# A grouped-query attention kernel: 480 rows of the output projection's weights loaded early through five transfer engines, the rest behind the last V block

## Chip, cores and metric

One core of a Trainium2 chip. The metric is device time of one execution in microseconds (us). The four runs of the kernel before agree within 0.2% (190.00 to 190.34 us).

## The reference, cut

```python
B, Sq, D = 8, 4, 512;  Hq, Hkv, Sk, Dh = 32, 8, 2048, 128      # all bf16
q = (x @ wq)                          # x: 32 tokens x 512, wq: 512 x 4096
scores = q . k_cache * Dh ** -0.5     # four query heads share one K/V head
o = softmax(scores) . v_cache         # k_cache, v_cache: 32 MiB each
return o.reshape(B, Sq, Hq * Dh) @ wo # wo: 4096 x 512, 4 MiB
```

## The kernel before: what the change and the argument touch

K and V come in 32 blocks of 1 MiB each, through one queue, into 7 and 6 buffers. Units are pairs of K/V heads: `p` is the head pair (four of them, `G2 = 4`), `b` the batch. The four quarters of `wo` belong to the four head pairs. `wo_sb` takes the buffer of `wq_sb`, so it can be loaded only after the queries are made. The trace shows sixteen completion increments for every load of 128 partitions; I read them as one for each of the core's sixteen transfer engines.

```python
def load_wo(p, r0, n):                 # r0..r0+n of 8 rows per partition
    rows = wo[p * HP * 128 : (p + 1) * HP * 128, :].rearrange("(q r) j -> q r j", r=WR)
    nc.sync.dma_start(wo_sb[:, p, r0 : r0 + n, :], rows[:, r0 : r0 + n, :])

load_k(0); <wq>; <x>
for u in range(NU + KA):               # the order of the loads
    if 0 < u < NU:                       loads.append(("k", u))
    if u >= KA - 1 and u - KA + 1 < NU:  loads.append(("v", u - KA + 1))
    if u in (NU, NU + 1):                # first quarter and half of the second
        loads.append(("wo", (u - NU, 0, WR if u == NU else 4)))
# ... [cut] identities, transposes of x and K, queries, scores, values ...
for step in range(-L - 1, NH):         # NH = 64 half blocks
    # ... [cut]
    if step == NH - 1 - 2 * VB:          # behind the last V block
        load_wo(1, 4, 4)
        load_wo(2, 0, WR)
        load_wo(3, 0, 4); load_wo(3, 4, 2); load_wo(3, 6, 2)
    if step == NH - 5:   project(0, 0, WR)
    elif step == NH - 3: project(1, 0, 4)
to_tokens(3);  project(1, 4, 4);  to_wo_rows(3)
project(2, 0, WR);  project(3, 0, 4);  project(3, 4, 2);  project(3, 6, 2)
# ... [cut] two copies (VectorE, ScalarE) and two stores
```

`project(p, r0, n)` is one matmul for each row of a partition and each half of the 512 output columns: `project(2, 0, WR)` is 16 matmuls.

The softmax here doesn't subtract the row's maximum and nothing guards it: scores larger than these inputs give would overflow.

## Time and profile before

| | before |
|---|---|
| time, median of 4 runs | 190.18 us (190.00 to 190.34) |
| span of the profiled run | 188.3 us |
| 1 MiB load of the third wo quarter lands | 181.68 us |
| last load of wo lands | 184.16 us |
| after that 1 MiB landing | 32 matmuls 3.67 us, a copy 0.36 us, the store |
| bytes read from memory | 72 MiB |

The prediction below shows the lines of the page. Two things are needed to read them. The span is shorter than the time of a run (187.7 against 189.51 us in the changed kernel's profiled run), because it counts from the first to the last instruction of the profile. And a load of 128 partitions has landed with the last of its sixteen completion increments (for the third wo quarter at 181.68 us, and its matmuls start at 181.72); the differences between the increments show how far the engines are apart. Where I print such differences, they come from these completion records, in an ordinary block.

### The profile page before, as it was taken

How to read it: one execution, taken by the hardware profiler on the slowest of the kernel's cores; microseconds unless marked ns; L12 is line 12 of the kernel's file. 1: busy time of each engine (PE TensorE's matmuls, PEld its weight loads, DVE VectorE, ACT ScalarE, POOL GpSimd, SP SyncE). 2: the span in 40 equal slices, each digit the busy share in tenths (PEclk: the TensorE clock that was granted, in tenths of full speed). 3: DMA queues.
4: the chain of work that ended last, by engine and by line, in shares of the span. 5: the costliest groups of instructions: out<-in, count | busy, mean ns of one | idle time of the engine just before them, and what ended most of it. 6: DMA issues, size and time to landing. Idle time of an engine off the chain costs nothing.

```text
span 188.3 us, 6428 instructions
## 1 busy us (share of the span) xinstructions
PE 154.9 (82%) x2861; PEld 141.9 (75%) x2892; DVE 113.3 (60%) x220; ACT 86.3 (46%) x170; POOL 1.1 (1%) x8
## 2 busy tenths in 40 slices
PE   0706597799999999998888889998885999998783
PEld 0605497699999898898888878887774988987572
DVE  6801544577777677767666668676664477673420
ACT  2011546665655666446554544454553464461000
POOL 2000000000000000000000000000000000000000
PEclk9985869999999999999999999999999699999999
DMA  6999999999999999999999999999999999999950
GB/s 251 425 438 393 418 430 426 423 428 425 419 425 421 426 421 423 430 419 423 431 421 421 430 423 421 425 426 425 423 421 428 425 426 423 426 424 416 422 207 10
DMA packets 10539, 75.97 MB, mean 403 GB/s; under 512 B 1200, under 2 KB 1296, under 8 KB 1936
## 3 DMA queue, kind: packets, MB, share of 16 engines
q1 hardware_dynamic: 10464, 75.55, 95.6%
q8 instruction: 22, 0.36, 0.7%
q14 instruction: 5, 0.04, 0.1%
q10 hardware_dynamic: 48, 0.02, 0.0%
HBM read 75.53 MB, written 0.03 MB: 401 GB/s over the span
## 4 chain that ended last, share of the span: by engine, by line
DMA 81%; PE 12%; ACT 3%; DVE 2%; issue 1%; SPq 1%; DVEq 0%
DMA k_sb<-in_k_cache_dram 64%; DMA wo_sb<-in_wo_dram 9%; DMA x_sb<-in_x_dram 7%; PE kp L161 3%; PE s_ps L222 3%; PE psq L185 2%; PE out_ps L314 2%; DVE kt L168 1%; ACT kt L166 1%; PE o_ps L246 1%; DVE q_bd L209 1%; ACT q_bd L209 1%; ACT probs L232 1%; PE l_ps L260 0%; PE pse L200 0%
## 5 line engine op out<-in xcount | busy, mean ns | idle before, releaser
L161 PE MATMUL kp<-ident,k_sb 128*128 128x128 f32 x512 | 83.1, 290 | 13.4 <-DMA k_sb<-in_k_cache_dram 13.4
L168 DVE COPY kt<-kp 128x1024 bf16<-128x1024 bf16 x96 | 65.3, 682 | 25.6 <-PE kp L161 24.9
L232 ACT ACTIVATE probs<-s_ps 64x256 bf16<-64x256 f32 x128 | 48.4, 378 | 66.3 <-PE s_ps L222 65.5
L161 PEld LDWEIGHTS kp<-ident,k_sb 128*128 128x128 f32 x512 | 56.7, 146 | 14.4 <-issue 14.1
L222 PE MATMUL s_ps<-q_bd,kt 128*128 128x64 bf16 x1024 | 43.3, 195 | 3.1 <-ACT kt L166 1.9
L222 PEld LDWEIGHTS <-kt 128*128 128x128 bf16 x1024 | 40.7, 100 | 4.9 <-ACT kt L166 2.2
L246 PEld LDWEIGHTS <-v_sb 128*128 128x128 bf16 x1024 | 34.4, 96 | 9.6 <-DMA v_sb<-in_v_cache_dram 2.4
L268 DVE TENSOR_REDUCE l_sb<-l_ps 128x32 f32<-128x512 f32 x32 | 22.1, 692 | 24.0 <-PE l_ps L260 21.7
L246 PE MATMUL o_ps<-probs,v_sb 128*128 128x32 bf16 x1024 | 35.1, 177 | 1.2 <-DMA v_sb<-in_v_cache_dram 1.1
L166 ACT COPY kt<-kp 128x1024 bf16<-128x1024 bf16 x32 | 32.4, 1012 | 8.1 <-PE kp L161 7.3
L260 PE MATMUL l_ps<-probs,ones 128*128 128x512 bf16 x33 | 12.4, 380 | 1.5
L272 DVE RECIPROCAL r_sb<-l_sb 128x32 f32<-128x32 f32 x32 | 11.3, 353 | 1.1
L314 PE MATMUL out_ps<-wo_sb,oP 128*32 128x256 bf16 x64 | 7.6, 272 | 0.8 <-DMA wo_sb<-in_wo_dram 0.8
L314 PEld LDWEIGHTS <-oP 128*32 128x32 bf16 x64 | 6.1, 96 | 1.5 <-issue 0.6
L367 ACT CAST out_sb<-out_ps 32x256 bf16<-32x256 f32 x1 | 0.4, 362 | 14.5 <-PE out_ps L314 14.5
L277 DVE TENSOR_TENSOR oT_all<-o_ps,r_sb 128x32 bf16<-128x32 f32 x32 | 5.8, 182 | 1.7 <-PE o_ps L246 1.5
L260 PEld LDWEIGHTS <-ones 128*128 128x128 bf16 x64 | 6.0, 98 | 0.8 <-issue 0.4
L176 PE MATMUL xtp<-ident,x_sb 32*128 32x32 bf16 x4 | 0.5, 191 | 6.6 <-DMA x_sb<-in_x_dram 6.4
L176 PEld LDWEIGHTS <-x_sb 32*128 32x128 bf16 x4 | 0.3, 114 | 7.1 <-DMA x_sb<-in_x_dram 6.8
L192 ACT ACTIVATE qT_all<-psq 128x256 bf16<-128x256 f32 x4 | 1.5, 386 | 8.7 <-PE psq L185 8.7
L209 DVE CAST q_bd<-pse 64x512 bf16<-64x512 f32 x4 | 2.6, 683 | 4.2 <-PE pse L200 4.2
L179 DVE COPY xT_sb<-xtp 128x32 bf16<-128x32 bf16 x4 | 0.5, 170 | 7.0 <-PE xtp L176 7.0
(23 smaller groups left out, 33.3 us busy)
## 6 DMA issues: line engine op xcount, KB each, us to landing
k_sb<-in_k_cache_dram SPq DMA_DIRECT2D x32, 1024.0 KB, 19.6
v_sb<-in_v_cache_dram SPq DMA_DIRECT2D x32, 1024.0 KB, 19.6
wq_sb<-in_wq_dram SPq DMA_DIRECT2D x1, 4096.0 KB, 14.2
wo_sb<-in_wo_dram SPq DMA_DIRECT2D x2, 1024.0 KB, 18.5
wo_sb<-in_wo_dram SPq DMA_DIRECT2D x3, 512.0 KB, 17.2
wo_sb<-in_wo_dram SPq DMA_DIRECT2D x2, 256.0 KB, 13.2
x_sb<-in_x_dram SPq DMA_DIRECT2D x1, 32.0 KB, 14.0
out_dram<-out_sb SPq DMA_DIRECT2D x1, 16.0 KB, 1.4
```

Of the source, the lines that this page charges most:

```text
L161: nc.tensor.transpose(kp[:, j, :], k4[:, w : w + 128], ident4[:, :])
L166: nc.scalar.copy(out=kt2, in_=kp2)
L168: nc.vector.tensor_copy(out=kt2, in_=kp2)
L209: (nc.scalar.copy if g else nc.vector.tensor_copy)(out=q_bd[rows, p, :, :, g, :], in_=pse[rows, :, :, :])
L222: nc.tensor.matmul(s_ps[:, 2 * j : 2 * j + 2, :], lhsT=k_t[:, j % (HC // 4), :, e], rhs=q_bd[:, p, e, b, :, :], start=(e == 0), stop=(e == 1),
L232: nc.scalar.activation(out=pr[rows, hf * HC : (hf + 1) * HC, cols], in_=s_ps[rows, :, cols], func=EXP)
L246: nc.tensor.matmul(o_ps[u][:, :], lhsT=vs[u][:, cc, :], rhs=pr[:, cc, :], start=(cc == 0), stop=(cc == C - 1),)
L260: nc.tensor.matmul(l_ps[:, :, :], lhsT=ones[:, :], rhs=pr[:, c : c + LC, :], start=(c == 0), stop=(c + LC == C),)
L268: nc.vector.tensor_reduce(out=l_sb[:, :], in_=l_ps[:, :, :].rearrange("d c q -> d q c"), axis=AX, op=ADD)
L272: nc.vector.reciprocal(r_sb[:, :], l_sb[:, :])
L277: nc.vector.tensor_tensor(out=oT_all[:, p * HP : (p + 1) * HP, b, :], in0=o_ps[u][:, :].rearrange("d (h s) -> d h s", h=HP), in1=r_sbs[u][ ...
L314: nc.tensor.matmul(out_ps[half][:, :], lhsT=oP[p][:, r, :], rhs=wo_sb[:, p, r, half * DH : (half + 1) * DH], start=(p == 0 and r == 0), st ...
```

## The change

The intent: the sixteen transfer engines drift apart during the run (increments 0.64 us apart at the third K block, 4.94 at the last load of wo), one more of them falling back by some 1.5 us at each of the first eight 16 KiB instruction fetches, and the end of the kernel waits for the slowest. So the first quarter of `wo` is used as ballast. Of its 1024 rows, 480 are loaded by eight small loads between the first K blocks, each of only 5 partitions and meant for only five engines; the rest goes behind the last V block. The early rows are projected in the middle of the kernel.

```diff
+    NE, WE, WM = 40, 12, 4                     # 40 partitions x 12 rows, 128 x 4, 32 x 1
+    wo_e = const.tile([64, WE, D], BF16, name="wo_e")
+    def load_wo_e(i):                          # five partitions, 12 KiB in each
+        hi, m = divmod(i, 4)
+        rows = wo[: NE * WE, :].rearrange("(q r) j -> q r j", r=WE)
+        a, b = hi * 32 + m, hi * NE // 2 + m
+        nc.sync.dma_start(wo_e[a : a + 17 : 4, :, :], rows[b : b + 17 : 4, :, :])
 ...
     for u in range(NU + KA):
+        if 1 <= u <= 8:
+            loads.append(("e", u - 1))
 ...
-        if u in (NU, NU + 1):
-            loads.append(("wo", (u - NU, 0, WR if u == NU else 4)))
 ...
+    nc.gpsimd.memset(wo_e[:, :, :], 0.0)       # ahead of the identities
     load_ready(0, 0)
 ...
         if step == NH - 1 - 2 * VB:
-            load_wo(1, 4, 4)
+            nc.sync.dma_start(wo_n[:, :], wo[HP * 128 - 32 : HP * 128, :])
+            load_wo_m()
+            load_wo(1, 0, WR)
             load_wo(2, 0, WR)
 ...
-        if step == NH - 5:
-            project(0, 0, WR)
-        elif step == NH - 3:
-            project(1, 0, 4)
+        if 28 <= step < 36:
+            e, r = divmod(step - 28, 4)
+            project_early(1 - e, r * 3, 3)
+        if step == 31:
+            nc.vector.tensor_copy(out=early[:, :], in_=out_e[:, 1, :])
     to_tokens(3)
-    project(1, 4, 4)
+    project(0, 0, WM + 1)
     to_wo_rows(3)
+    project(1, 0, WR)
     project(2, 0, WR)
 ...
-    nc.scalar.copy(out=out_sb[1][:, :], in_=out_ps[1][:, :])
+    nc.vector.tensor_tensor(out=out_sb[1][:, :], in0=out_ps[1], in1=early[:, :], op=ADD)
```

Cut here: the tiles `wo_m`, `wo_n`, `oE`, `oM`, `oN`; the exchange of the two last copies and stores between ScalarE and VectorE; the transposes that bring the first head pair into the new row order; the four transposes of x, which now share one PSUM tile and one copy; the PSUM pools (one buffer for the values instead of two, one for the early projection); and two unused tiles (`pad0`, `pad`) that keep the start addresses of the large tiles at multiples of 512 bytes.

More of the change, by code (lines that the diff above doesn't have):

```diff
@@ L47 @@
     DH = D // 2
+    NE, WE, WM = 40, 12, 4
+    assert NE * WE + 128 * WM + 32 == HP * 128
     AX = mybir.AxisListType.X
@@ L60 @@
     psum_s = ctx.enter_context(tc.tile_pool(name="psum_s", bufs=2, space=bass.MemoryType.PSUM))
-    psum_o = ctx.enter_context(tc.tile_pool(name="psum_o", bufs=2, space=bass.MemoryType.PSUM))
+    psum_o = ctx.enter_context(tc.tile_pool(name="psum_o", bufs=1, space=bass.MemoryType.PSUM))
+    psum_e = ctx.enter_context(tc.tile_pool(name="psum_e", bufs=1, space=bass.MemoryType.PSUM))
     psum_l = ctx.enter_context(tc.tile_pool(name="psum_l", bufs=1, space=bass.MemoryType.PSUM))
     order = ctx.enter_context(tc.manual_schedule())
+    pad0 = const.tile([128, 192], BF16, name="pad0")
+    wo_e = const.tile([64, WE, D], BF16, name="wo_e")
+    wo_n = const.tile([32, D], BF16, name="wo_n")
+    wo_m = const.tile([128, WM, D], BF16, name="wo_m")
     x_sb = const.tile([T, D], BF16, name="x_sb")
@@ L77 @@
     out_sb = [const.tile([T, DH], BF16, name=f"out_sb{i}") for i in range(2)]
-    oP = [const.tile([128, WR, T], BF16, name=f"oP{p}") for p in range(G2)]
+    oP = [None] + [const.tile([128, WR, T], BF16, name=f"oP{p}") for p in range(1, G2)]
+    oE = const.tile([64, WE, T], BF16, name="oE")
+    oM = const.tile([128, WM, T], BF16, name="oM")
+    oN = const.tile([32, T], BF16, name="oN")
+    early = const.tile([T, DH], FP32, name="early")
     ident = const.tile([128, 128], BF16, name="ident")
     ones = const.tile([128, 128], BF16, name="ones")
-    pad = const.tile([128, 64], BF16, name="pad")
+    pad = const.tile([128, 96], BF16, name="pad")
     probs = [const.tile([128, C, NQ], BF16, name=f"probs{i}") for i in range(L // 2 + 2)]
@@ L106, in load_v, with load_wo_m @@
         )
+    def load_wo_e(i):
[3 more added lines that the diff above has]
+        nc.sync.dma_start(wo_e[a : a + 17 : 4, :, :], rows[b : b + 17 : 4, :, :])
+    def load_wo_m():
+        nc.sync.dma_start(
+            wo_m[:, :, :], wo[NE * WE : HP * 128 - 32, :].rearrange("(q r) j -> q r j", r=WM)
+        )
     def load_wo(p, r0, n):
         rows = wo[p * HP * 128 : (p + 1) * HP * 128, :].rearrange("(q r) j -> q r j", r=WR)
-        nc.sync.dma_start(wo_sb[:, p, r0 : r0 + n, :], rows[:, r0 : r0 + n, :])
+        nc.sync.dma_start(wo_sb[:, p - 1, r0 : r0 + n, :], rows[:, r0 : r0 + n, :])
     load_k(0)
@@ L128, in load_ready @@
             kind, u = loads[-1]
-            if kind == "wo":
+            if kind == "e":
                 loads.pop()
-                load_wo(*u)
+                load_wo_e(u)
                 continue
@@ L173 @@
             transpose_part(i, part)
+    xtp = psum_o.tile([128, R, T], BF16, tag="o", name="xtp")
     for r in range(R):
-        xtp = psum_o.tile([128, T], BF16, tag="o", name="xtp")
         nc.tensor.transpose(
-            xtp[:, :], x_sb[:, :].rearrange("t (p r) -> t r p", r=R)[:, r, :], ident[:T, :T]
+            xtp[:, r, :], x_sb[:, :].rearrange("t (p r) -> t r p", r=R)[:, r, :], ident[:T, :T]
         )
-        nc.vector.tensor_copy(out=xT_sb[:, r, :], in_=xtp[:, :])
+    nc.vector.tensor_copy(out=xT_sb[:, :, :], in_=xtp[:, :, :])
     for p in range(G2):
@@ L211 @@
             )
-    wo_sb = wpool.tile([128, G2, WR, D], BF16, tag="w", name="wo_sb")
+    wo_sb = wpool.tile([128, G2 - 1, WR, D], BF16, tag="w", name="wo_sb")
     def scores(i):
@@ L301, in to_wo_rows, with project_early @@
     def to_wo_rows(p):
-        perm = psum_l.tile([128, WR, T], BF16, tag="l", name="perm")
-        for r in range(WR):
-            nc.tensor.transpose(
-                perm[:, r, :],
-                nats[p][:, :, :].rearrange("t q r -> t r q")[:, r, :],
-                ident[:T, :T],
+        flat = nats[p][:, :, :].rearrange("t q r -> t (q r)")
+        if p > 0:
+            perm = psum_l.tile([128, WR, T], BF16, tag="l", name="perm")
+            rows = flat.rearrange("t (q r) -> t r q", r=WR)
+            for r in range(WR):
+                nc.tensor.transpose(perm[:, r, :], rows[:, r, :], ident[:T, :T])
+            nc.vector.tensor_copy(out=oP[p][:, :, :], in_=perm[:, :, :])
+            return
+        perm = psum_l.tile([128, WE + WM + 1, T], BF16, tag="l", name="perm")
+        rows = flat[:, : NE * WE + 12 * WE].rearrange("t (q r) -> t r q", r=WE)
+        for r in range(WE):
+            for hi in range(2):
+                q0 = hi * NE // 2
+                nc.tensor.transpose(
+                    perm[hi * 32 : hi * 32 + 32, r, :], rows[:, r, q0 : q0 + 32], ident[:T, :T]
+                )
+        rows = flat[:, NE * WE : HP * 128 - 32].rearrange("t (q r) -> t r q", r=WM)
+        for r in range(WM):
+            nc.tensor.transpose(perm[:, WE + r, :], rows[:, r, :], ident[:T, :T])
+        nc.tensor.transpose(perm[:32, WE + WM, :], flat[:, HP * 128 - 32 :], ident[:T, :T])
+        nc.vector.tensor_copy(out=oN[:, :], in_=perm[:32, WE + WM, :])
+        nc.vector.tensor_copy(out=oE[:, :, :], in_=perm[:64, :WE, :])
+        nc.vector.tensor_copy(out=oM[:, :, :], in_=perm[:, WE : WE + WM, :])
+    def project_early(half, r0, n):
+        for r in range(r0, r0 + n):
+            nc.tensor.matmul(
+                out_e[:, half, :],
+                lhsT=oE[:, r, :],
+                rhs=wo_e[:, r, half * DH : (half + 1) * DH],
+                start=(r == 0),
+                stop=(half == 1 and r == WE - 1),
             )
-        nc.vector.tensor_copy(out=oP[p][:, :, :], in_=perm[:, :, :])
     def project(p, r0, n):
@@ L313, in project @@
             for r in range(r0, r0 + n):
+                if p > 0:
+                    o, w = oP[p][:, r, :], wo_sb[:, p - 1, r]
+                else:
+                    o, w = (oN[:, :], wo_n) if r == 0 else (oM[:, r - 1, :], wo_m[:, r - 1])
                 nc.tensor.matmul(
-                    out_ps[half][:, :],
-                    lhsT=oP[p][:, r, :],
-                    rhs=wo_sb[:, p, r, half * DH : (half + 1) * DH],
-                    start=(p == 0 and r == 0),
+                    out_ps[half],
+                    lhsT=o,
+                    rhs=w[:, half * DH : (half + 1) * DH],
+                    start=(half == 1 and p == 0 and r == 0),
                     stop=(p == G2 - 1 and r == WR - 1),
@@ L349 @@
             load_wo(3, 6, 2)
-        if step == NH - 5:
-            out_ps = [
-                psum_s.tile([T, DH], FP32, tag="s", name=f"out_ps{n}") for n in range(2)
-            ]
-            project(0, 0, WR)
-        elif step == NH - 3:
-            project(1, 0, 4)
+        if step == 28:
+            out_e = psum_e.tile([T, 2, DH], FP32, tag="e", name="out_e")
+        if 28 <= step < 36:
[3 more added lines that the diff above has]
+            nc.vector.tensor_copy(out=early[:, :], in_=out_e[:, 1, :])
+    out_ps = [out_e[:, 0, :], psum_s.tile([T, DH], FP32, tag="s", name="out_ps")[:, :]]
     to_tokens(3)
-    project(1, 4, 4)
+    project(0, 0, WM + 1)
     to_wo_rows(3)
+    project(1, 0, WR)
     project(2, 0, WR)
@@ L365 @@
     o2 = out.flatten_outer_dims()
-    nc.vector.tensor_copy(out=out_sb[0][:, :], in_=out_ps[0][:, :])
-    nc.scalar.copy(out=out_sb[1][:, :], in_=out_ps[1][:, :])
-    nc.sync.dma_start(out=o2[:, :DH], in_=out_sb[0][:, :])
-    nc.scalar.dma_start(out=o2[:, DH:], in_=out_sb[1][:, :])
+    nc.scalar.copy(out=out_sb[0][:, :], in_=out_ps[0])
+    nc.vector.tensor_tensor(out=out_sb[1][:, :], in0=out_ps[1], in1=early[:, :], op=ADD)
+    nc.scalar.dma_start(out=o2[:, :DH], in_=out_sb[0][:, :])
+    nc.sync.dma_start(out=o2[:, DH:], in_=out_sb[1][:, :])
 _INS = ['x', 'k_cache', 'v_cache', 'wq', 'wo']
```

## The prediction

The sum came to -1.14 + 0.05 = about -1.1 us, 190.28 to 189.2, and stands, but part of the terms it comes from is cut. The missing step of (1): 8 x 12 = 96 KiB of early rows on each of five engines, with 34 KiB from the other loads 130 instead of 64 KiB (+66), and 34 (-30) on the other eleven; at 0.038 us per KiB these are the +2.51 and -1.14 us. The bytes per engine are divisions. That each early load uses five engines, the same five each time, was assumed: the kernel before has no load of 5 partitions to show it. From R1 an estimate: with an engine of two fetches among the five, the end of the spread would be 3.08 + 2.51 = 5.59 us, 0.65 later than 4.94, and the time 190.9.

> **What bounds the kernel now.** I read the page first: slices, queues, chain of waits. The lines that carry it:
>
> ```profile
> DMA  6999999999999999999999999999999999999950
> GB/s 251 425 438 393 418 430 426 423 428 425 419 425 421 426 421 423 430 419 423 431 421 421 430 423 421 425 426 425 423 421 428 425 426 423 426 424 416 422 207 10
> ...
> q1 hardware_dynamic: 10464, 75.55, 95.6%
> q8 instruction: 22, 0.36, 0.7%
> ...
> DMA 81%; PE 12%; ACT 3%; DVE 2%; issue 1%; SPq 1%; DVEq 0%
> ```
>
> The transfer engines are 90% busy or more in slices 1 to 37, at a flat 420 to 430 GB/s, and the chain that ended last is 81% transfers. No compute engine is close: the busiest, the matmul row, is at 82% only because its records overlap. So this kernel is a stream of 72 MiB (32 K blocks, 32 V blocks, 4 MiB of wq, 4 MiB of wo) with a tail. Next the waits of the queue that issues the loads, and the end of the chain:
>
> ```profile
> SPq L103 <- DMA v_sb<-in_v_cache_dram: 54.4, 25, 3.7
> SPq L93 <- DMA k_sb<-in_k_cache_dram: 48.7, 24, 3.6
> ...
> SPq L103 <- PE o_ps L246: 6.8, 4, 2.9
> ```
>
> ```profile
> 164.40 17.27 DMA wo_sb<-in_wo_dram
> 181.68 0.04 issue
> 181.72 3.67 PE out_ps L314 x32
> 185.38 0.02 issue
> 185.41 0.36 ACT out_sb L367
> ```
>
> The issuer mostly waits for transfers themselves (eight completion semaphores are used in turn, so eight loads are in flight), hardly for buffers. The end: a 1 MiB load of wo lands at 181.68, 32 projection matmuls follow without a gap at 3.67/32 = 0.115 us each, then a copy (0.36) and the store. The last wo load lands at 184.16 (completion records), before those matmuls are through, so the end is set by the landing of the 1 MiB load of wo plus 32 matmuls.
>
> A load has landed only when its slowest transfer engine is done. The trace keeps all sixteen completion increments of every load, without the engine's name. Their offsets from the first, in us:
>
> ```
> third K block   (lands at 20.4):  0 to 0.27 (8 of them), 0.40 to 0.64 (8)
> fourth K block  (lands at 24.3):  the same, but one at 2.16
> last wo load    (lands at 184.16): 0 0.04 0.10 0.57 0.67 0.77 1.42 1.75 2.83 3.08 4.68 4.76 4.79 4.91 4.92 4.94
> ```
>
> So the sixteen engines do not finish together: at the end the first is 4.94 us ahead of the last. The cause is on the page: 22 instruction fetches, each a 16 KiB packet of about 0.94 us. At each one (33.0, 43.2, 52.5 on the trace's own clock, and so on) one more engine falls back by some 1.5 us, and after eight fetches the turn begins again. 22 = 6 x 3 + 2 x 2: six engines have three fetches (offsets 4.68 to 4.94), two have two (2.83, 3.08), and eight have none (0 to 1.75, two of them set back by smaller 8 KiB fetches). The mean offset is 40.2/16 = 2.5, so a perfect balance would save 4.94 - 2.5 = 2.4 us and no more. That is what the change goes after.
>
> [...]
>
> **The change part by part.** (1) Bytes. Before, the first 1 MiB of wo put 64 KiB on each engine. [...] the 512 rows in 128 partitions put 32 KiB and the 32 rows in 32 partitions 2 KiB on every engine. [...] The other eleven: 34 KiB, -30. A 1 MiB load is 64 KiB per engine and landings follow each other at 2.435 us, so 0.038 us per KiB: +2.51 us on five engines, -1.14 us on eleven. If the five are the five that lead, their offsets become 2.5 to 3.2, and the six slow ones 3.54 to 3.80: the last landing is 4.94 - 3.80 = 1.14 us earlier.
>
> (2) Start. GpSimd now zeroes wo_e (6,144 elements a partition) before the identities.
>
> ```profile
> masks.py:197 POOL MEMSET ident<- 128x128 bf16 (+1 forms) x2 | 0.4, 205 | 0.3 <-POOLq L384 0.3
> L384 POOL MEMSET const-bfloat16-1.0<- 128x1 bf16 x1 | 0.1, 102 | 0.0
> ```
>
> From 1 to 128 elements the duration grows by 103 ns, 0.8 ns an element; 6,144 take about 5 us (an estimate from these two rows). The identities are then ready near 6.7 instead of 1.8, and the first K transposes start near 6.7 instead of 5.66. VectorE's copies of the identity and its memsets (0.62 + 1.76 + 0.17 + 2.65) end near 11.7, three K copies of 0.69 near 13.8. x lands at 15.65 behind 4 MiB of wq, so all of it stays hidden by almost 2 us. The issuer waits for the memset too, until about 6, but 5 MiB (k0 and wq, 12 us) are then in the queue.
>
> (3) Flow. Of eight loads in flight, up to three are now 60 KiB ones, so the early depth falls from about 8 MiB to 5 MiB, still 12 us of transfer, more than any engine's lead. During the first 35 us the five engines fall behind by about 3 us and blocks land that much later. Compute is not what the stream waits for there, and the K and V pools hold 13 blocks.
>
> (4) Matmul work: 34 projection matmuls for the first wo quarter instead of 16, and 21 more small transposes: (18 + 21) x about 0.1 = 4 us, spread over the middle where the array has slack; off the path. One PSUM buffer for o_ps instead of two makes the next block's values wait for VectorE's 0.18 us product; between them lie transposes, scores and norms of about 2 us, so hidden.
>
> (5) Tail. V31 lands earlier relative to the end: 0.53 + 1 + 1 + 1 MiB follow it, 8.6 us instead of 2.5 MiB = 6.1. Rows of the first and second quarter (10 and 16 matmuls, 1.1 and 1.8 us) fit between the landings. The last two quarters keep their order and sizes, so the end is still "1 MiB landing + 32 matmuls". The final VectorE step adds two operands instead of a copy and comes last: I allow +0.05.
>
> Sum: -1.14 + 0.05 = about -1.1 us, 190.28 to 189.2.
>
> **The rivals.** R1: the five are not the leaders. Nothing in the trace names an engine. [...] If an engine with three fetches is among the five: 4.94 + 2.51 = 7.45, 2.5 later: 192.8. R2: a stall in the start (a memset slower than the estimate, or the shallower queue) opens a hole in the stream. For: the identities are on the way of all transposes. Against: 12 us of queued bytes. If the memset took 12 us instead of 5, compute would start 4 to 5 us late, and the pools would about absorb it: 0 to +1.5 us. R3: the balance does not count because something else ends last, for instance projection matmuls piling up: then 190.3. Against it is the gapless 32 at the end, which start at the landing.
>
> **Range and chances.** 0.6 for the balance as intended (189.0 to 189.7, smaller if the five include one set back to 1.75), 0.2 for an outcome near no change (189.7 to 191), 0.2 for slowed engines among the five or a hole (191 to 193). I predict 189.3 us, a little above the pure sum, with 8 in 10 between 188.6 and 191.4. A 2% change is 3.8 us, above the 2.4 that perfect balance could give, and above the 2.5 that the worst choice of engines costs: faster 0.01, same 0.96, slower 0.03.
>
> **What would show it.** Right: the last wo loads' increments spread over about 3.8 us instead of 4.9, the 1 MiB wo landing near 180.6, 32 matmuls after it, the 5-partition loads with 5 late increments; GB/s flat from slice 1. Wrong engines: a spread of 5.6 or 7.5 at the end. A start problem: a slice under 400 GB/s among the first eight, or kp waiting past 15 us. Another bound: a gap or a different wait ahead of the last 32 matmuls.

## The result, and the profile after

The changed kernel took 189.82 us (189.51, 189.81, 189.84, 189.98), the kernel before on the same chip 190.18 (190.00 to 190.34). Ratios here are the mean time of one kernel's fast runs over that of the other's in the same rounds, so not quite the ratio of the medians: 0.9979, with a 95% interval of 0.9962 to 0.9997. That is 0.36 us less by the medians, where I had expected 1.0. The profiled span went from 188.3 to 187.7 us; the profiled run of the changed kernel (189.51 us) is the fastest of its four, the other three have spans of 187.9 to 188.1 us.

The page of the changed kernel: granted clock, transfer share and GB/s in 40 slices, the queues (packets, MB, share of the engines' time), the shares of the chain that ended last, and the row of the new memset (busy us, mean ns, idle before it).

```profile
PEclk9995769999999999999999999999999999999999
DMA  6999999999999999999999999999999999999960
GB/s 209 461 447 382 423 436 418 429 425 426 420 424 421 419 431 421 419 436 419 422 429 421 424 429 419 424 421 428 424 424 426 422 428 424 421 429 417 413 271 8
...
q1 hardware_dynamic: 10448, 75.55, 96.0%
q8 instruction: 23, 0.38, 0.7%
...
DMA 92%; issue 3%; PE 2%; POOL 0%; SPq 0%; DVE 0%; POOLq 0%
...
L164 POOL MEMSET wo_e<- 64x6144 bf16 x1 | 5.2, 5211 | 0.3 <-POOLq L447 0.3
```

The stream is as flat as before, 413 to 436 GB/s in slices 5 to 38; slice 4 is at 382 (before 393). The memset takes 5.21 us. What the array and the issuing queue wait for at the start (waits: us in total, times, the longest):

```profile
PE kp L188 <- POOL ident masks.py:199: 7.0, 1, 7.0
...
SPq L127 <- POOL ident masks.py:197: 4.6, 1, 4.6
```

The first K transposes wait for the identities until 7.0 us, and the issuer waits 4.6 us for GpSimd; neither leaves a hole in the stream. The end of the chain (start, duration, what):

```profile
164.98 0.02 issue
165.00 16.04 DMA wo_sb<-in_wo_dram
181.04 0.04 issue
181.08 1.03 PE out_e L371 x8
182.12 0.87 PE out_ps L371 x8
182.99 0.44 PE out_e L371 x4
183.43 0.44 PE out_ps L371 x4
183.86 0.22 PE out_e L371 x2
184.08 0.22 PE out_ps L371 x2
184.30 0.22 PE out_e L371 x2
184.52 0.23 PE out_ps L371 x2
184.75 0.02 issue
184.77 0.41 DVE out_sb L430
```

It is the same end as before: the 1 MiB load lands, 32 matmuls run without a gap (181.08 to 184.75, 3.67 us as before), one small step on VectorE (0.41 against ScalarE's 0.36), the store. From that landing to the end of the span it is 6.7 us in both kernels. So the whole gain of the profiled span is the landing: 181.68 to 181.04, 0.64 us less. Why not 1.14? The completion increments of the last load of wo, offsets from the first in us:

```
before (first at 179.22, last at 184.16):
  0 0.04 0.10 0.57 0.67 0.77 1.42 1.75 | 2.83 3.08 | 4.68 4.76 4.79 4.91 4.92 4.94
after  (first at 178.28, last at 183.57):
  0 0.18 0.51 | 2.81 3.07 | 4.42 4.46 4.51 4.56 4.60 4.62 | 3.54 3.55 4.26 4.94 5.28   (the loaded five put last)
```

The six engines with three instruction fetches now end 1.25 us earlier (before, at up to 184.16; after, at 178.28 + 4.62 = 182.90), about the 1.14 predicted for their smaller share of wo. But they are not last any more. The last is one of the five loaded engines, 0.66 us behind them. How the five came to stand apart shows at four K blocks of the changed kernel, the five largest offsets of each:

```
landing at  50.53:  3.54 3.57 3.58 3.63 3.68
landing at  56.33:  3.55 3.56 3.57 3.67 4.57
landing at  66.04:  3.55 3.56 3.66 4.40 4.47
landing at 125.86:  3.56 4.31 4.37 5.41 (and another engine at 3.55)
```

At 50 us all ballast is in, and the five stand together, 3.54 to 3.68 us behind the leader. 96 KiB more than the others at 0.038 us per KiB (1 MiB lands every 2.435 us, 64 KiB for each engine) are 3.65: the rate of the prediction is right. Then single ones of them fall back by some 0.6 to 1 us, at about 51, 60, 119 and 122 us, where the small queue of 8 KiB instruction fetches (5 packets in the whole run) has its packets. Three of the five have fallen back by 125.86 us. They look like the engines that stood at 0.77, 1.42 and 1.75 before: with 3.65 added that gives 4.42, 5.07 and 5.40, and 4.26, 4.94 and 5.28 were measured. The trace does not name engines, so that these are the same ones is inferred from the sizes.

The 0.64 us is also the best of three profiles. Two other profiles of this program have an undisturbed stream (e_same below, and e_addr, where only an unused tile is wider). There the same load lands at 181.36 and 181.38 us, only 0.3 us earlier than before, and the five engines stand 3.5 to 4.0 us behind the leader already at the K block that lands at 50.8 us. That is nearer to the 0.36 us of the medians. Why the five stand up to 0.3 us further back in one run than in another is not shown.

### The profile page after: what moved, and what is told of

It reads as the page before. It is cut to its first block, busy times and chain, and to the rows that moved or that the text cites. A ratio compares the mean times of both kernels' runs of the same rounds, so it can differ in the third digit from the quotient of the medians.

```text
span 187.7 us, 6524 instructions
## 1 busy us (share of the span) xinstructions
PE 159.3 (85%) x2931; PEld 142.2 (76%) x2931; DVE 113.7 (61%) x220; ACT 86.2 (46%) x170; POOL 6.3 (3%) x9
## 4 chain that ended last, share of the span: by engine, by line
DMA 92%; issue 3%; PE 2%; POOL 0%; SPq 0%; DVE 0%; POOLq 0%
DMA k_sb<-in_k_cache_dram 62%; DMA wo_e<-in_wo_dram 13%; DMA wo_sb<-in_wo_dram 9%; DMA v_sb<-in_v_cache_dram 8%; PE out_e L371 1%; PE out_ps L371 1%; DVE out_sb L430 0%; SPq L107 0%; POOL ident masks.py:197 0%; POOL ident masks.py:199 0%; SPq L127 0%; POOL wo_e L164 0%; POOLq masks.py:199 0%; POOLq L447 0%
## 5 line engine op out<-in xcount | busy, mean ns | idle before, releaser
L188 PEld LDWEIGHTS kp<-ident,k_sb 128*128 128x128 f32 x512 | 55.9, 144 | 18.0 <-POOL ident masks.py:199 7.0
L249 PE MATMUL s_ps<-q_bd,kt 128*128 128x64 bf16 x1024 | 42.3, 194 | 3.0 <-ACT kt L193 1.9
L249 PEld LDWEIGHTS <-kt 128*128 128x128 bf16 x1024 | 39.9, 99 | 4.7 <-ACT kt L193 2.2
L287 PE MATMUL l_ps<-probs,ones 128*128 128x512 bf16 x64 | 19.0, 379 | 0.0
L371 PEld LDWEIGHTS <-oP 128*32 128x32 bf16 x48 | 4.6, 97 | 1.0 <-issue 0.4
L164 POOL MEMSET wo_e<- 64x6144 bf16 x1 | 5.2, 5211 | 0.3 <-POOLq L447 0.3
L171 DVE COPY pick<-ident 128x64 bf16<-128x64 bf16 x4 | 0.6, 220 | 6.5 <-POOL ident masks.py:199 6.5
L356 PE MATMUL out_e<-wo_e,oE 64*32 64x256 bf16 x24 | 4.0, 272 | 0.0
L212 PE MATMUL psq<-xT_sb,wq_sb 128*128 128x32 bf16 x128 | 3.6, 188 | 0.3 <-DVE xT_sb L206 0.3
L212 PEld LDWEIGHTS <-wq_sb 128*128 128x128 bf16 x128 | 3.6, 104 | 0.3 <-issue 0.3
```

The lines of the kernel that those rows point to most:

```text
L188: nc.tensor.transpose(kp[:, j, :], k4[:, w : w + 128], ident4[:, :])
L212: nc.tensor.matmul(psq[:, h, :], lhsT=wq_sb[:, r, hh * 128 : (hh + 1) * 128], rhs=xT_sb[:, r, :], start=(r == 0), stop=(r == R - 1),)
L249: nc.tensor.matmul(s_ps[:, 2 * j : 2 * j + 2, :], lhsT=k_t[:, j % (HC // 4), :, e], rhs=q_bd[:, p, e, b, :, :], start=(e == 0), stop=(e == 1),
L287: nc.tensor.matmul(l_ps[:, :, :], lhsT=ones[:, :], rhs=pr[:, c : c + LC, :], start=(c == 0), stop=(c + LC == C),)
L371: nc.tensor.matmul(out_ps[half], lhsT=o, rhs=w[:, half * DH : (half + 1) * DH], start=(half == 1 and p == 0 and r == 0), stop=(p == G2 - 1 ...
```

## The experiments

Theory A: the gain is the balance of the engines alone, and it is limited by those of the five that carry small instruction fetches. Rival B: the gain has another source, the shorter order of loads or the early projection, and the same bytes spread over all sixteen engines give it too. Rival C: the ballast is too small, and more of it moves the end further. When the first runs came in, two more questions arose: why the changed kernel itself was often slower than the kernel before in later jobs, and what sets off a slow phase of the transfers. Kernels of one job share a chip and the runs of the kernel before. All runs gave correct results.

### The changed kernel again (e_same), ballast on sixteen engines (e_spread), more ballast (e_heavy), less (e_light)

The edits, cut to the sizes:

```diff
 # e_same: none
 # e_spread
-    NE, WE, WM = 40, 12, 4
+    NE, WE, WM = 128, 4, 4        # early: 128 partitions x 4 rows, in two loads
 # e_heavy
-    NE, WE, WM = 40, 12, 4
+    NE, WE, WM = 40, 16, 3        # 16 KiB in each of the 40 partitions
 # e_light
-    NE, WE, WM = 40, 12, 4
+    NE, WE, WM = 40, 11, 4        # 11 KiB; 72 more rows behind the last V block
```

> The changed kernel once more, as the base for the other runs. Theory A (each transfer engine ends at its own sum of loaded bytes and instruction fetches, and the one with the largest sum sets the end; after the change that is one of the five loaded engines that also carries two of the 8 KiB fetches): 0.4 to 0.6 us under the kernel before (189.6 to 189.9), last load's increments spread over 5.2 to 5.4 us. Rival B (the gain comes from the rearranged tail and the early projection) and rival C (the six engines with three 16 KiB fetches still set the end) expect the same time here.

> Same early projection and same tail order, but the early rows (512) go to 128 partitions, so each of the 16 engines carries 64 KiB of this quarter as before the change. Theory A: the gain is gone, 190.2 to 190.3 against 190.2 of before, last load's increments spread over 4.9 us as before. Rival B: the gain stays, 189.7 to 189.9.

> 640 early rows instead of 480 on the same five engines: 152 KiB each instead of 130, 24 instead of 34 on the others. Theory A: 22 KiB x 0.038 = 0.84 us later than the changed kernel, so 190.5 to 190.7, spread of the last load 5.28 + 0.84 + 0.38 = 6.5 us. Rival C (the three-fetch engines set the end): 10 KiB x 0.038 = 0.4 us earlier than the changed kernel, 189.3 to 189.5.

> 440 early rows instead of 480: 125 KiB on the five, 36.5 on the others. Theory A: 5 KiB x 0.038 = 0.2 us earlier than the changed kernel (189.5 to 189.7), spread 5.28 - 0.2 - 0.1 = 5.0 us. Rival C: 0.1 us later than the changed kernel, 189.9 to 190.0.

Measured: e_spread 192.97 us (192.58 to 193.03), e_heavy 192.69, e_light 192.66, against 190.0 for the kernel before. All three were slower by 2.7 to 3.0 us, which neither theory had. GB/s of e_spread's page:

```profile
GB/s 206 453 439 365 422 427 417 424 418 420 417 412 418 420 415 417 422 418 415 422 417 422 418 417 422 417 415 418 417 420 420 420 418 417 420 418 415 409 206 9
```

The stream is slower everywhere: the mean of slices 6 to 37 is 418.5 GB/s, and 424.2 in the kernels before and after. The packets of 8 KiB took 316.5, 315.8 and 316.7 ns on average in the three, and 311.1 and 311.6 in the kernels before and after. What the three share is that my new sizes moved all tiles behind `wo_e`: K, V and the wo buffer start past a multiple of 512 bytes, by 448 in e_spread, 128 in e_heavy and 448 in e_light, where the kernel before and the changed one start at a multiple. Against the 311.1 ns of the kernel before their packets took 1.7 and 1.8% longer at a remainder of 448 bytes and 1.5% longer at 128. By what mechanism is not shown. That the addresses are the cause is: in the next job e_spread2 differs from e_spread in the width of an unused tile alone, and takes 190.41 us (median, on another chip, the kernel before at 190.0 in both jobs) instead of 192.97. So these three tell nothing about the balance by their time. By their spread they do: offsets of the last load end at 4.98 us (spread over sixteen: no balance), 7.11 (more ballast) and 5.45 (less). This was a fault of my experiments, and the unused tiles of the change are there for just this.

The changed kernel itself (e_same) gave 189.63, 189.98, 192.3, 192.36, 193.47 and 194.0 in one job, against 189.87 to 190.13 of the kernel before. The profiled run is the one of 192.3. Its granted clock and GB/s:

```profile
PEclk9995869999999999999999999999999999999669
...
GB/s 212 449 440 399 422 429 422 429 424 434 415 421 421 423 427 416 435 418 427 425 423 423 430 423 420 428 420 425 425 425 421 427 423 425 428 421 417 366 89 7
```

The transfers are as in the good run: the third quarter lands at 181.36, the last load at 183.82. But the clock row ends in 669. Stretches of the end, first of the good run of the changed kernel, then of this one (stretch; its length; busy us of PE, PEld, DVE, ACT and POOL with instructions; clock; transfer share; GB/s):

```profile
173.60:177.00 3.40, 2.07 (x43) 1.40 (x41) 1.52 (x5) 0.00 (x0) 0.00 (x0) 1.00 1.02 418
177.00:180.40 3.40, 3.40 (x32) 2.61 (x32) 0.88 (x2) 0.00 (x0) 0.00 (x0) 1.00 0.87 360
180.40:183.80 3.40, 3.14 (x29) 2.64 (x28) 0.00 (x0) 0.00 (x0) 0.00 (x0) 1.00 0.45 174
```

```profile
173.60:177.00 3.40, 2.01 (x50) 1.42 (x45) 1.68 (x5) 0.00 (x0) 0.00 (x0) 1.00 1.02 416
177.00:180.40 3.40, 3.40 (x24) 1.83 (x22) 0.87 (x2) 0.00 (x0) 0.00 (x0) 0.57 0.87 362
180.40:183.80 3.40, 3.40 (x18) 2.39 (x17) 0.10 (x1) 0.00 (x0) 0.00 (x0) 0.50 0.47 179
```

From 177.44 to 184.27 us (the trace's clock record) the array ran at half its clock, just where 26 projection matmuls and 8 transposes wait behind the last V block and 32 more follow: 18 matmuls instead of 29 in the third stretch. The end is then set by the array, not by a landing, and comes 2.8 us later. Before the drop the array was busy in 2.01 of the first 3.40 us shown, waiting for the last V block (1.10 us) and more; the good run has 2.07 there and kept its clock. But these stretches are not the clock's own. In the clock record the clock changes in steps of 3.41 us, and the last whole step before the drop holds 2.02 us of busy array here (174.03 to 177.44), 2.07 in e_same2 and 2.10 in e_addr, which lost the clock too. The step at that place in the good run (174.28 to 177.69) holds 2.40. What sets off the drop is not shown. The granted clock in it is 0.50, and it lasts 6.83 us, two of these steps. The steps fall differently over the same work in the good run and in the slow one, so that it may be chance how they fall: a guess. Steps with 59 to 62% busy time came before the drop in three profiles, but busy time alone does not decide it: e_spread2 kept its clock after a step with 2.08 us (174.92 to 178.33). Theory T of the next expectations is my guess from the one profile of e_same.

### The control again (e_same2), spare matmuls (e_warm), and two aligned sizes (e_spread2, e_light2)

```diff
 # e_warm: in the loop, step == NH - 2, ahead of values(step): the last V block
+                spare = psum_k.tile([128, HC // 4, 128], FP32, tag="k", name="kp")
+                for _ in range(5):
+                    nc.tensor.matmul(spare[:, :, :], lhsT=ones[:, :],
+                                     rhs=q_bd[:, 0, 0, :, :, :], start=True, stop=True)
 # e_spread2, e_light2: e_spread and e_light with a wider unused tile
-    pad = const.tile([128, 96], BF16, name="pad")
+    pad = const.tile([128, 896], BF16, name="pad")      # e_light2: 640
```

> The changed kernel again, as control. In the last job 4 of 6 runs took 192.3 to 194.0, 2 took 189.6 and 190.0; the profiled slow one had its loads landing as early as the fast one, but its matmuls ran at half clock from 177.4 to 184.3. Theory T (while the array waits for the last V block it is too little busy, and loses its clock for two stretches of 3.4 us when the stretch falls badly): again two groups, 189.5 to 190.0 and 192 to 194. Rival R (that job met a bad chip): all runs 189.5 to 190.0.

> Five idle matmuls of 512 columns (about 1.1 us, result never read) put before the last V block's values, where the array waits about 1.1 to 1.3 us. Theory T: the half-clock stretch at the end is gone, all runs 189.5 to 190.0. Rival R: the same share of slow runs as the control.

> e_spread again, with the pad widened so that K and V tiles start at a multiple of 512 bytes as in both kernels (in e_spread, e_heavy and e_light they did not, and their 8 KiB packets took 316 ns instead of 311). Theory A: no gain from balance, fast runs 190.1 to 190.3 (half-clock runs above 192 apart), last load's increments spread over 4.9 to 5.0 us, third-quarter wo load landing near 181.7. Rival B (gain from tail and early projection): fast runs 189.6 to 189.9.

> e_light again, aligned the same way, all addresses of K and V as in the changed kernel. Theory A: five loaded engines 5 KiB lighter, so 0.2 us earlier than the changed kernel: fast runs 189.4 to 189.7, spread 5.0 us. Rival C (three-fetch engines set the end): 0.1 us later, 189.8 to 190.1.

Measured: e_same2 189.74 once, and 192.04 to 194.63 five times; the kernel before 189.96 to 190.25 in eleven runs. So the changed kernel loses its small gain more often than not on this chip. e_warm, for which I had expected 189.5 to 190.0 throughout: 189.96, 190.19, 190.38, 190.68, and 192.1 and 194.12. Its profile fell on the run of 192.1:

```profile
PEclk9999979999999999999999999999999999999999
DMA  6999999999999999999999999999999999999960
GB/s 217 444 441 377 390 392 383 391 399 423 423 413 430 418 430 418 430 420 427 424 424 425 425 420 429 424 420 427 424 425 425 422 429 424 420 429 418 408 254 8
```

The clock holds to the end in this run, as intended, but even the four better runs show no gain over the kernel before. In the profiled run the time is lost elsewhere: slices 5 to 9, about 16 to 42 us, run at 383 to 399 GB/s instead of 418 to 436. There the 8 KiB packets take 342 ns instead of 309, without any queue being empty. The profiled run of e_same2 (194.63) has both, 342 ns from 16 to 42 us and the half clock at the end. I call the first the slow transfer phase.

e_spread2 took 190.14 to 190.76 (kernel before 190.0), its third quarter lands at 182.28, the last load at 184.74, with a spread of 4.92. With nearly the same early rows (512 instead of 480) and the same tail, but the ballast spread evenly, nothing is gained. Rival B is out, theory A stands. e_light2 took 190.16 to 190.77, and once 193.66; I had expected 189.4 to 189.7. Its spread was 5.08 (expected 5.0), less than the 5.28 of the full ballast, as theory A has it, but the landing of the third quarter at 181.38 is no better than the 181.04 of the changed kernel, and its clock row has a 6 in slice 38. At this size (0.2 us) its time settles nothing.

### The old tail with the new balance (e_tail), the same with a cut load (e_tail_split), ballast later (e_late), more ballast aligned (e_heavy2)

```diff
 # e_tail: 512 + 32 rows of the first and half the second quarter between the last V blocks again
+        if u in (NU, NU + 1):
+            loads.append(("w", u - NU))
 ...
+        if step == NH - 5:
+            project(0, 0, WM + 1)
+        elif step == NH - 3:
+            project(1, 0, 4)
 # e_tail_split: e_tail, and
-            load_wo(2, 0, WR)
+            load_wo(2, 0, 4)
+            load_wo(2, 4, 4)
 ...
-    project(2, 0, WR)
+    project(2, 0, 4)
+    project(2, 4, 4)
 # e_late: the changed kernel, with the ballast at K blocks 13 to 20
-        if 1 <= u <= 8:
+        if 13 <= u <= 20:
 # e_heavy2: e_heavy with a wider unused tile
```

> The changed kernel, but the remaining wo rows of the first quarter and half of the second go back between the last V blocks and their projection between the last blocks' work, as in the kernel before; early loads and their five engines stay. Theory T (the half clock at the end comes from the thin matmul work after the last V block was moved forward): no half-clock stretch after 150 us in the profile, fast runs 189.5 to 189.9, none at 192.0 to 192.6 with a clock of 0.955; what is left above 191.5 is the slow transfer phase. Rival R: half-clock runs as often as before the edit.

> e_tail with the 1 MiB load of the third quarter in two halves, so that its first 8 matmuls do not wait for all of it. The last matmuls then end 0.45 us after the last landing instead of 1.2: fast runs 0.6 to 0.7 us under e_tail, 188.8 to 189.3. If the array's backlog were not what follows the landing: as e_tail.

> The eight 5-partition loads go between K blocks 13 to 20 instead of 1 to 8, the early projection 16 half-blocks later. In some runs of the changed kernel all 8 KiB packets took 342 ns instead of 309 from 16 to 42 us (2.4 us lost). Theory S (these loads in the stream cause it): slow runs at 191.9 to 192.6 remain, the slow phase then lies at 50 to 110 us. Theory V (something of the start causes it: fewer bytes in flight, late issue): no slow phase later; if it is still at 16 to 42 us without any 5-partition load there, these loads are cleared. Fast runs 189.5 to 190.0.

> e_heavy again (640 early rows) with K and V tiles at a multiple of 512 bytes. Theory A: last load's spread 6.5 to 7.1 us, fast runs 190.4 to 190.8. Rival C (three-fetch engines set the end): 189.3 to 189.5. Half-clock and slow-phase runs lie 2 us and more above either.

Measured, with the kernel before in this job at 189.98 to 190.33 in ten runs and once at 192.72:

- e_tail: 189.78, 189.84, 189.94, 189.95, and 192.42 and 194.13. The four are the time of the changed kernel's good runs. The profiled 194.13 has the full clock to the end and the slow transfer phase from 16 to 62 us:

```profile
GB/s 252 430 412 392 386 384 395 389 388 391 384 392 385 409 424 433 418 423 431 421 424 426 424 423 424 426 416 426 426 426 423 424 426 424 417 417 410 413 265 8
```

- e_tail_split: 189.26, 189.32, 189.38, 189.40, and 192.91 and 193.97 (the profiled one, again with the slow phase, 16 to 62 us). I had expected 188.8 to 189.3. In its undisturbed runs it beats both kernels: their mean is 189.34, 0.7 us less than the kernel before in this job (median 190.03) and 0.45 less than the changed kernel (189.79, of its own job).
- e_late: 190.12, 190.13, 190.74, 190.95, 190.95, 193.56. The profiled run (190.95) has packets of 352 ns at 16 to 22 us, though no 5-partition load is anywhere near. So the phase can come without these loads; its longer forms, to 42 or 62 us, were seen only in profiles of kernels that have them early. The best two runs, 190.12 and 190.13, also miss the expected 189.5 to 190.0.
- e_heavy2: 190.25, 190.29, 190.6, 190.64, 191.28, 194.32; expected by theory A were 190.4 to 190.8, by rival C 189.3 to 189.5. Two of the six lie just under theory A's range, none near rival C's. The spread was 6.75 (expected 6.5 to 7.1). More ballast makes the end later: rival C is out.

### The start alone (b_memset), ballast late and identities first (e_late_id), other addresses (e_addr), the cut load alone (b_split)

```diff
 # b_memset: the kernel before, ahead of the identities
+    for _ in range(6):
+        nc.gpsimd.memset(oT_all[:, :, :, :], 0.0)
 # e_late_id: e_late with the memset of wo_e behind the identities
 # e_addr: the changed kernel; K, V and wq tiles at the same remainder of 8 KiB as before
-    pad = const.tile([128, 96], BF16, name="pad")
+    pad = const.tile([128, 2656], BF16, name="pad")
 # b_split: the kernel before
-            load_wo(2, 0, WR)
+            load_wo(2, 0, 4)
+            load_wo(2, 4, 4)
 ...
-    project(2, 0, WR)
+    project(2, 0, 4)
+    project(2, 4, 4)
```

> The kernel before, with nothing but six GpSimd memsets of 1,024 elements ahead of the identities, on a tile that is written long after; no address moves. The identities and K transposes are then some 5 us late, as in the changed kernel. If the late start sets off the slow transfer phase (8 KiB packets of 340 ns and more from 16 us on), about a third of the runs or more are at 191 to 194 us. If it does not, all are at 190.0 to 190.4, like the kernel before, which was slow once in about 48 runs. The end does not change in either case.

> The 5-partition loads between K13 and K20, and the memset after the identities: loads and identities then start as in the kernel before. If the late start is what sets off the slow phase, no run shows it: all at 189.6 to 190.3, with packets of 309 ns at 16 to 22 us. If it is something else (tile addresses, the chip), two or three of six runs are over 190.7. The last spread stays near 5.3 us.

> The changed kernel with a wider unused tile, so that the K, V, wq and wo tiles start at the same remainders of 4 and 8 KiB as in the kernel before (in the changed kernel they start 1 KiB off a 2 KiB multiple). If these addresses set off the slow phase or the half clock, all runs are at 189.5 to 190.0. If they don't matter, it is a third changed kernel with two or more of six over 191 us.

> The kernel before with only the 1 MiB load of the third wo quarter cut into two halves and its projection with it: 16 of the 32 last matmuls (1.84 us) can then run before the second half lands at 181.7, and the end follows the last landing (184.2) plus 4 matmuls (0.46 us) or the second half plus 32 matmuls less 16. I expect 189.4 to 189.7 us, so that most of the gain of the best version comes without the change at all. If 190.0 or more, the gain needs the change's balance.

Measured (kernel before 189.99 to 190.32 in ten runs, once 191.19):

- b_memset: 189.96 to 190.29 in five runs, once 192.41. The late start costs the kernel before nothing (190.05 median of the five), and the slow run in six is no third, so the late start is not shown to set anything off.
- e_late_id: 189.94 to 190.25 in five runs, once 191.75. Also no clear answer: one slow run in six. And its gain is gone, at undisturbed runs of about 190.2. In its profile the landings are 181.41 and 183.94, but the array runs without a gap from 177.44 to 185.50 and is itself the end (in the changed kernel it began the same transposes at 176.25). That the later ballast and early projection make it late is likely, but was not tried by itself.
- e_addr: 192.38, 192.03, 192.41, 192.32, 190.67, 189.72. The addresses don't matter. Its profile (192.38) shows the half clock at the end again and no slow phase.
- b_split: 189.62, 189.68, 189.69, 189.79, and 191.89 and 193.87. Two changed lines in the kernel before already give 0.4 us in the undisturbed runs. I expected 189.4 to 189.7. The end of its chain says why it isn't more:

```profile
159.47 18.43 DMA v_sb<-in_v_cache_dram
177.95 0.98 PE o_ps L246 x32
178.95 0.20 DVE oT_all L277
179.20 0.62 PE nat L289 x8
179.82 0.87 PE out_ps L314 x8
180.69 0.60 PE perm L304 x8
181.29 3.61 PE out_ps L314 x32
184.92 0.36 ACT out_sb L369
```

Once the 1 MiB load is cut, the end is no more a landing of wo but that of the last V block and the array's work behind it, again 32 matmuls in a row, from 181.29 instead of 181.72.

### The kernel before as a tested kernel (b_same), and the change with a cut load and spare matmuls (e_split_warm)

```diff
 # b_same: none against the kernel before
 # e_split_warm: the changed kernel with e_warm's five matmuls and the cut of e_tail_split
```

> The kernel before itself, unchanged, in the place of a tested kernel. As the reference of its jobs it was over 190.5 us in 2 of 48 runs; kernels tested beside it, even the one with only a cut load, in about a third. If that share belongs to the kernels, all six runs here are at 190.0 to 190.4. If it belongs to the place in a job or the loading of a program, one to three of six are at 191 to 194 us.

> The changed kernel, its wo loads still behind the last V block, with the third wo quarter's load cut into halves and five spare matmuls ahead of the last V block's values against the half clock. From the landings of the changed kernel (halves of the quarter at 179.8 and 181.04, then 182.31, 182.94, 183.57) and 0.11 us a matmul the last matmul ends at 184.2 instead of 184.75: 189.2 to 189.5 us in its fast runs, about as the version with the early rows moved back (189.39), and no half clock at the end. If the last V block's chain is what ends last, 189.7 or more.

b_same: 189.95 to 190.21 in five runs, once 191.13. Together with its runs as the reference, the kernel before was over 191 us in 3 of about 65 runs, the worst 192.72. e_split_warm: 189.44, 189.44, 189.51, and 190.7, 192.86 and 193.86. The best three are as expected (189.2 to 189.5, at its upper edge), but the reason is not. I had the last matmul end at 184.2; the chain of the profiled run (189.51, no slow phase, full clock):

```profile
176.68 0.62 PE nat L316 x8
177.31 0.75 PE out_e L371 x5
178.05 0.75 PE out_ps L371 x5
178.80 0.59 PE perm L334 x8
179.39 0.98 PE out_e L371 x8
180.37 0.87 PE out_ps L371 x8
181.25 0.44 PE out_e L371 x4
...
184.30 0.22 PE out_e L371 x2
184.52 0.23 PE out_ps L371 x2
184.78 0.41 DVE out_sb L442
```

The array runs without a gap from 176.68 on, 48 matmuls of the last three quarters from 179.39, and the last ends at 184.75, to the hundredth where it ended in the changed kernel. So the work behind the last V block is the end here, not a landing. That the end is the same does not mean that the cut is worth nothing: in this run the loads land later than in the changed kernel's profile (the two halves at 180.26 and 181.49, the last load at 183.96 instead of 183.57). Uncut, 32 matmuls (3.67 us) behind the landing at 181.49 would end near 185.16, an estimate, so the cut saves some 0.4 us. Where those rows are back between the V blocks, the same cut brings 0.5 us (e_tail 189.88, e_tail_split 189.34, means of the four undisturbed runs).

### The sum of the runs

| kernel | undisturbed runs, us | others, us |
|---|---|---|
| before | 190.00 to 190.34 | |
| changed | 189.51 to 189.98 | none of 4 |
| changed (e_same, e_same2, e_addr) | 189.63, 189.72, 189.74, 189.98 | 190.67, 13 from 192.03 to 194.63 |
| ballast spread evenly (e_spread2) | 190.14 to 190.76 | |
| with full clock at the end (e_warm) | 189.96 to 190.68 | 192.1, 194.12 |
| old tail (e_tail) | 189.78 to 189.95 | 192.42, 194.13 |
| cut load alone (b_split) | 189.62 to 189.79 | 191.89, 193.87 |
| balance, old tail, cut load (e_tail_split) | 189.26 to 189.40 | 192.91, 193.97 |

Runs with the half clock are about 1.3% longer than the good runs, just inside the bound of 1.5% under which a run of one core counts as fast. So the ratios of these jobs mix both (e_same 1.0057, e_addr 1.007), and I list the runs instead. Undisturbed is judged by the time, because only one run of each kernel has a profile, and the line is not sharp: 190.67 stands under others, 190.68 and 190.76 do not.

## Why the prediction was right or wrong

**The bound.** Right. The stream sets the end through the landing of the 1 MiB load, with the same 32 gapless matmuls (3.67 us) behind it; the gain of the profiled span, 0.6 us, is the 0.64 us of that landing. (The words "a flat 420 to 430 GB/s" for slices 1 to 37 are loose: the line shows 393 to 438. And the matmul row's 82% is already the union of its records: 512 transposes of K at 290 ns each make 148 us, and the page counts 83.1. So overlap is not why it is high; that the array was not the bound is shown by the end, where it waits for the landing.)

**The cause and the mechanism.** Right, in direction and rate. Five engines fell back by 3.54 to 3.68 us for 96 KiB (3.65 by the prediction's rate), the six slow ones came 1.25 us earlier (predicted 1.14), and the even spread gained nothing. Each 5-partition load shows one increment at once and five late ones (the first load: one at 7.20 us, five from 15.4 to 15.6): the five late increments that the prediction had asked for.

**The step that failed** is in "The change part by part", (1): "If the five are the five that lead, their offsets become 2.5 to 3.2, and the six slow ones 3.54 to 3.80: the last landing is 4.94 - 3.80 = 1.14 us earlier." The five were engines without the large fetches, but not the five that lead: by the sizes, two of them are the ones set back to 1.42 and 1.75 by the small 8 KiB fetches (and a third, at 0.77, has one such fetch, which the prediction did not count). On the scale of that sentence the worst becomes 1.75 + 2.51 = 4.26 instead of 3.2, so the last landing is 4.94 - 4.26 = 0.68 us earlier; 0.59 was measured for the last load and 0.64 for the one that counts, in the fastest run; 0.3 in e_same and e_addr, and 0.36 by the medians. So what was mis-sized is the offset that the loaded engines end with: 3.2 at most by the prediction, 4.26 by this sum, and 4.94 - 0.59 = 4.35 by the last landing. The text has this case in half a sentence ("smaller if the five include one set back to 1.75"), without working it out, and put the weight on the other. Nothing in the trace told which engines were which, but the number of candidates was known: five of the eight engines without large fetches, two of which are set back. To miss both by chance, all five would have to come from the other six: 6 of 56 ways if any five were equally likely. The case that I called the exception was the likely one. That no engine with a large fetch was among the five was not known beforehand either; the prediction had named that risk.

**The start.** Right: memset 5.21 us (estimate 5), K transposes from 7.0 (6.7), no hole in the stream. A late start by itself costs nothing (b_memset, 190.05 us in the median of its five undisturbed runs).

**The tail.** Right for the undisturbed runs, incomplete otherwise. "Rows of the first and second quarter (10 and 16 matmuls, 1.1 and 1.8 us) fit between the landings" holds at full clock, barely: in e_split_warm the array has no gap from 176.68 us on. At half clock it does not hold, and the end moves to the array; that is R3, "projection matmuls piling up", with a cause that I had not thought of and a cost of 2.2 to 2.8 us. In three later jobs 13 of 18 runs of the changed kernel were at 192 us or more, and part of that is this. With the work taken out of the tail (e_tail, e_tail_split) or the array kept busy (e_warm, e_split_warm) 8 of 24 were over 191.5, and each of the four profiles showed a full clock at the end. That is strong but not complete: only one run of each kernel has a profile, and of the four only e_warm shared a chip with the changed kernel (2 of 6 runs over 191.5 us there, against 5 of 6). That all four runs on record were undisturbed was luck, or their chip.

**R1, R2.** No engine with a large fetch is among the five (the two-fetch ones are still at 2.81 and 3.07), and no hole opened at the start. The range, 188.6 to 191.4, held the result, but it was wide enough to hold no change at all (190.2); the class (within 2%) is right too.

**What stays open.** What sets off the slow transfer phase from 16 us on. It starts where wq has landed (15.5 us in the changed kernel's trace) and ends at about 22, 42 or 62 us, mostly near an instruction fetch (21.6, 41.3, 59.7 and 60.5 us in that trace). In it the packets of 8 KiB took 342 ns (e_warm, e_same2) and 352 ns (e_late) instead of 309, and slices 5 to 9 of e_warm ran at 383 to 399 GB/s instead of 418 to 436. It came without the 5-partition loads (e_late, 16 to 22 us), and is not shown to be the late start (b_memset, 1 slow run in 6, without a profile of it) or the addresses (e_addr). All six profiles that have it come from two of the chips used. The kernel before was seen slow rarely, yet with two lines changed in its tail (b_split) it was slow in 2 of 6 runs. Those two have no profile, so whether this phase belongs to the change stays open too.

## What to carry to other kernels

Where a load waits for the slowest of sixteen engines, ballast on a few of them shifted the balance here, at 0.038 us per KiB (3.54 to 3.68 us for 96 KiB); but first find, from the completion increments, what each engine carries, small fetches included, and size the gain by the worst of the engines that get the ballast. Look at what the array has to do between the last large block and the end before putting more behind it: at full clock the work here fitted, at half clock (18 matmuls instead of 29 in 3.40 us) it was the end, 2.8 us later. So keep that stretch short (e_tail, e_tail_split) or the array busy (e_warm, e_split_warm): each of these four profiles showed a full clock to the end. In undisturbed runs, cutting the one load that the end waits for was worth as much here (0.4 us for two lines) as the balance (0.36), and the two together 0.7; and when sizes change in an experiment, check that tile addresses kept their alignment (packets of 315.8 to 316.7 ns instead of 311.1 made these kernels 2.7 to 3.0 us slower).
